# First FFN product of six chunks in three pairs by Strassen's scheme, with a new order

## The chip, the cores and the metric

The kernel runs on one core of a Trainium2 chip. The metric is the device time of one execution in microseconds; smaller is better. The engines are TensorE (PE: matmuls, and PEld for its weight loads), VectorE (DVE), ScalarE (ACT), GpSimd (POOL) and SyncE (SP, which issues the DMAs). All run at once and meet at semaphores.

## The reference

A block-local attention is followed by a feed-forward network (FFN):

```python
# q, k, v: (4, 8, 768, 64); local window of 16 positions, plus 24 block summaries
k_sum = k.reshape(B, H, nb, 32, D).max(axis=3)
v_sum = v.reshape(B, H, nb, 32, D).mean(axis=3)
scores_l = where(|i - j| < 16, q @ k.T / sqrt(D), -1e9)
scores_s = q @ k_sum.T / sqrt(D) + log(32)
a = softmax(concat([scores_l, scores_s], -1))
x = (a @ concat([v, v_sum])).transpose(0, 2, 1, 3).reshape(3072, 512)
h = x @ w_in                      # (3072, 512) @ (512, 2048)
g = h / (1 + exp(-h))
out = g @ w_out                   # (3072, 2048) @ (2048, 512)
```

## The kernel before

**Tiling.** The 3072 tokens are 24 stages of 128 (s, six to each of four batches b) and 12 chunks of 256 (c, two stages each). The 2048 columns of w_in are 8 pairs of 128-wide f tiles (f below is such a pair; d is the tile in it). The contraction of 512 is four blocks of 128 (ct). Operands of the large products are split in two float16 parts, high and low, and a product is three matmuls: high x high, high x low, low x high.

**Attention of a stage.** `job_qk` and `job_vs` load and split q, k and v (DMA, ScalarE, VectorE). `job_a` (L645) makes the scores of a quad on TensorE (L681), adds mask and takes the minimum on VectorE (L692), the exponential on ScalarE (L695), scales and splits p (L267 to L277), and transposes p by DMA (L737). `job_c` multiplies by v, two stages at once (AV, L770). `job_x` (L778) brings x from PSUM as high part (ScalarE, L267) and low part (VectorE, L274).

**FFN of a step (c, f)**, `job_f` (L898). First product, L916: 2 d x 4 ct x 3 terms = 24 matmuls of 128x128 weights by 256 tokens, into one PSUM bank h (d side by side). Then tanh on ScalarE (L930), (tanh + 1) * h on VectorE (L931, `stt`), a float16 cast on ScalarE (L935, `cast`) and its rest on GpSimd or VectorE (L277, `less`). Second product, L925: per half of the chunk 2 d x 3 terms = 6 matmuls of 512 columns, accumulated over all f in one bank per half. The bank h alternates between 0 and 1 from step to step. In chunks 0 and 1 f runs in two parts and the second product is in float32 for the first.

**Banks.** 0 and 1: h. 4, 5 (and 2, 3): outputs. From b = 1 on the scores use 2 and 6, AV 3 and 7.

**Order.** No engine's order is the source's. Every operation is given to `Plan.op` (L87) with the engines that may run it, its cost and the keys it reads and writes. `Plan.replay` (L179) reads the string `ORDER` (L1038): three base-36 digits for an operation's number times five plus its engine (pe, dma, dve, act, pool). Each engine issues its operations in that order and waits at each until its inputs and its bank are ready. The x of chunks c + 2 is made during the steps of chunk c.

## Time and profile before

| | us |
|---|---|
| median of 3 runs | 613.48 (613.43 to 615.46) |
| profiled execution, its own time | 614.0 |
| its span, first to last instruction | 612.3 |
| TensorE busy | 606.2 (99%), clock 1.00 |
| VectorE / ScalarE / GpSimd busy | 414.1 (68%) / 368.3 (60%) / 137.6 (22%) |

Busy time counts an instruction from its start to its end; matmuls overlap each other, so their mean duration is longer than the distance from one to the next. The chain of waits goes back from the last instruction, at each step to what released it. The span of the first step of chunks 2, 6, 8 and 10 to the next gives the stages used below: chunk 2 begins at 141.0 us, chunk 6 at 330.7, chunk 8 at 427.4, chunk 10 at 518.5.

### The profile page before, as it was taken

The page shows a single profiled execution, that of the slowest core. Times are in us where ns is not written, and L with a number is a line of the kernel's source. Part 1 is how long each engine was busy: PE and PEld are TensorE (multiplying, and loading weights), DVE is VectorE, ACT ScalarE, POOL GpSimd, SP SyncE. Part 2 cuts the span into 40 slices and gives each one's busy share as a digit, 9 for nine tenths or more (in the row PEclk, how much of TensorE's full clock was granted, in tenths as well). Part 3 has the DMA queues.
Part 4 walks back from the last instruction along what each step waited for, and adds up shares of the span by engine and source line. Part 5 has one row for each costly group of instructions (what it writes and reads, how often), then busy time and mean ns, then how long its engine had stood idle before and what let it go on. Part 6 is the DMA issues. An engine that isn't in the chain of part 4 may idle for free.

```text
span 612.3 us, 13657 instructions
## 1 busy us (share of the span) xinstructions
PE 606.2 (99%) x5229; PEld 417.3 (68%) x5229; DVE 414.1 (68%) x1135; ACT 368.3 (60%) x839; POOL 137.6 (22%) x191
## 2 busy tenths in 40 slices
...
GB/s 303 346 363 414 240 73 128 141 222 89 186 121 113 148 178 130 138 185 96 132 140 145 154 175 102 164 129 150 119 171 50 57 109 117 40 27 57 39 15 35
DMA packets 85701, 87.89 MB, mean 144 GB/s; under 512 B 66796, under 2 KB 69100, under 8 KB 83588
## 3 DMA queue, kind: packets, MB, share of 16 engines
...
## 4 chain that ended last, share of the span: by engine, by line
PE 96%; DMA 2%; ACT 0%; SPq 0%; DVE 0%; issue 0%; DVEq 0%
PE bank L925 42%; PE bank L916 41%; PE bank L770 4%; PE bank L681 3%; PE bank L754 1%; DMA wt<-in_w_dram 1%; DMA wt<-in_kF_dram 1%; PE bank L673 1%; PE bank L676 1%; PE bank L704 0%; PE bank L389 0%; PE bank L706 0%; PE bank L799 0%; ACT e L695 0%; PE bank L856 0%; PE bank L461 0%
## 5 line engine op out<-in xcount | busy, mean ns | idle before, releaser
L925 PE MATMUL bank<-wt,g 128*128 128x512 f16 (+2 forms) x1168 | 276.6, 383 | 0.0
L916 PE MATMUL bank<-xh,wt 128*128 128x256 f16 x1536 | 272.1, 273 | 0.0
L916 PEld LDWEIGHTS <-wt 128*128 128x128 f16 x2304 | 223.8, 98 | 50.1 <-issue 5.1
L916 PE MATMUL bank<-xl,wt 128*128 128x256 f16 x768 | 209.3, 273 | 0.0
L925 PEld LDWEIGHTS <-g 128*128 128x128 f16 x1104 | 105.8, 98 | 101.0 <-issue 0.9
L930 ACT ACTIVATE t<-bank,asc 128x512 f32<-128x512 f32 x96 | 65.8, 686 | 128.2 <-PE bank L916 123.9
L931 DVE SCALAR_TENSOR_TENSOR t<-t,bank 128x512 f32<-128x512 f32 x96 | 65.7, 685 | 105.1 <-ACT t L930 105.0
L695 ACT ACTIVATE e<-e,mx 128x182 f32<-128x182 f32 x192 | 83.8, 438 | 32.5 <-DVE mx L692 32.0
L277 POOL TENSOR_TENSOR g<-t,g 128x512 f16<-128x512 f32 x45 | 52.6, 1169 | 215.7 <-ACT g L935 115.2
L935 ACT CAST g<-t 128x512 f16<-128x512 f32 x88 | 54.1, 615 | 43.0 <-DVE t L931 40.3
L692 DVE CUSTOM_DVE_ANT_0 e<-bank,masks,qsc 128x182 f32<-128x182 f32 x144 | 54.7, 401 | 16.3 <-PE bank L681 15.7
L274 DVE SCALAR_TENSOR_TENSOR p<-e,sum,p 128x182 f16<-128x182 f32 x160 | 60.6, 423 | 5.3 <-ACT p L267 2.6
L269 POOL TENSOR_SCALAR p<-e,sum 128x182 f16<-128x182 f32 x61 | 29.0, 480 | 149.1 <-DVE sum L714 29.7
L277 DVE TENSOR_TENSOR g<-t,g 128x512 f16<-128x512 f32 x43 | 29.8, 692 | 15.6 <-ACT g L935 15.5
L695 ACT ACTIVATION_READ_ACCUMULATOR e<-e,mx 128x1 f32 x192 | 36.1, 188 | 0.0
L770 PEld LDWEIGHTS <-vv 128*64 128x64 f16 x800 | 22.7, 110 | 2.7 <-issue 2.1
L770 PE MATMUL bank<-tt,vv 128*64 128x128 f16 x800 | 24.4, 220 | 0.0
L267 ACT ACTIVATE p<-e,sum 128x182 f16<-128x182 f32 x50 | 20.8, 437 | 4.8 <-DVE sum L714 1.7
L681 PE MATMUL bank<-qk 64*128 64x182 f16 x432 | 23.3, 239 | 0.0
L274 DVE SCALAR_TENSOR_TENSOR vv<-raw,vsc,vv 128x1024 f16<-128x1024 f32 x17 | 21.7, 1278 | 1.3 <-ACT vv L267 1.3
L681 PEld LDWEIGHTS <-qk 64*128 64x128 f16 x432 | 15.5, 94 | 10.1 <-issue 9.5
L830 POOL TENSOR_SCALAR wt<-wt 128x1024 uint32<-128x1024 uint32 x12 | 13.9, 1157 | 35.4 <-DMA wt<-in_w_dram 17.2
...
## 6 DMA issues: line engine op xcount, KB each, us to landing
...
```

Source lines behind the costliest of these rows:

```text
L269: nc.gpsimd.tensor_scalar(out=out, in0=in_, scalar1=by, scalar2=0.0, op0=ALU.mult, op1=ALU.add)
L274: nc.vector.scalar_tensor_tensor(out=out, in0=in_, scalar=by, in1=less, op0=ALU.mult, op1=ALU.subtract)
L277: eng[e].tensor_tensor(out=out, in0=in0, in1=in1, op=ALU.subtract)
L681: nc.tensor.matmul(out=bank[pair_banks[o]][:, i * 256:i * 256 + NKEY], lhsT=ql_or_h[pr, hp, :], rhs=kst[pr, j, hp, :], start=(n == 0), sto ...
L692: plan.op({"dve": 258 if b == 0 else 323}, lambda e, i=i: nc.vector.tensor_tensor_reduce(out=et[:, i, :NKEY], in0=sc[:, i, :NKEY], in1=mas ...
L695: plan.op({"act": 431}, lambda e, i=i, h=h: nc.scalar.activation(out=et[:, i, :NKEY], in_=et[:, i, :NKEY], func=AF.Exp, scale=-1.0, bias=m ...
L770: nc.tensor.matmul(out=to[j * D:(j + 1) * D, i * P:(i + 1) * P], lhsT=vs[w][:, vi, h * D:(h + 1) * D], rhs=tt[:, j * 3 + blk, :], start=(n ...
L916: nc.tensor.matmul(out=h[:, d * CH:(d + 1) * CH], lhsT=wt[f, 0][:, part, d, ct * P:(ct + 1) * P], rhs=x[:, ct, :], start=(ct == 0 and q == ...
L925: nc.tensor.matmul(out=bank[to][:, :z0 - a0], lhsT=a[:, d * CH + u * P:d * CH + u * P + P], rhs=b[:, d, a0:z0], start=(opens and d == 0 an ...
L930: plan.op({"act": 640}, lambda e: nc.scalar.activation(out=t, in_=h, func=AF.Tanh, scale=asc_t[c // 3 % 2][:, f:f + 1]), r=[("bank", k), ( ...
L931: plan.op({"dve": 605}, lambda e: nc.vector.scalar_tensor_tensor(out=t, in0=t, scalar=1.0, in1=h, op0=ALU.add, op1=ALU.mult), r=[("bank", ...
L935: plan.op({"act": 540}, lambda e: nc.scalar.copy(out=gh, in_=t), r=[("t", j)], w=[("gh", n)], prio=at - TUNE["post"])
```

## The change

Chunks 6 to 11 run in pairs (6, 7), (8, 9), (10, 11). With the two chunks as rows, the halves of the contraction, and the two f tiles, h of a step is a 2 x 2 by 2 x 2 block product, and it is made by seven block products M1 to M7 of two ct each (6 matmuls a product) in place of eight, in `pair_f`. M1 and M5 go to the bank of the first chunk (left); `out5` copies M5 to SBUF and M1 to the second chunk's bank (right); M6 accumulates there; add6 writes the left bank's other half; M7 accumulates; add7 writes the right bank's other half; M2 and M3 finish the left bank, M4 the right. Then both banks go through the same tanh, `stt`, `cast`, `less` (`post`) and second products as before, with six g buffers in place of three. Pairs 6-7 and 8-9 use banks 0 and 1 in every step; pair 10-11 alternates with 6 and 7. `pair_x` also keeps x in float32 and makes four block sums with their high and low parts; `sum_w` makes four block sums of w_in for each f. From stage 16 on scores and AV share banks 6 and 7. All x of a pair is made before its first step, during the pair before.

The new ORDER has 2563 operations (2362 before): TensorE 518 (500), VectorE 927 (837), ScalarE 692 (615), GpSimd 181 (164), DMA 245 (246). Decoded, TensorE's order at the start of pair 6-7 (3.n is the n-th step of that pair, in the f order of PORDER; M15 is M1 and M5, M23 is M2 and M3; f2 a second product, a or b its chunk, 0 or 1 its half; sc scores):

```
c5.7f1_0 c5.7f1_1 c5.4f2_0 c5.5f2_0 s15av c5.6f2_0 c5.6f2_1 c5.7f2_0 c5.7f2_1 3.0M15 3.0unit
3.0M6 3.0M7 3.0M23 3.0M4 3.1M15 3.0f2a1 3.1M6 3.0f2a0 3.1M7 3.1M23 3.1M4 3.0f2b0 3.2M15 3.1f2a0
3.2M6 s16qtr 3.2M7 s16sc 3.1f2b0 3.2M4 s16sc 3.2M23 3.1f2a1 s17sc 3.0f2b1 3.3M15
```

VectorE's there (xlo: low part of x; v2: split of v; km: block maximum of k, for which L440 loads kF):

```
3.0out5 3.0add6 3.0add7 s15xlo s16v2 3.0stta s16km 3.0lessa 3.0sttb 3.1out5 s16km 3.1add6 s16km 3.1add7
```

TensorE's at the start of pair 8-9 and of pair 10-11, and its end:

```
3.7f2b0 s19av 3.6f2a1 3.5f2a0 3.7f2a1 s20sc 4.0M15 3.6f2a0 4.0M6 s20sc 4.0M7 4.0M23 4.0M4 3.7f2a0 4.1M15
s21sc 4.1M6 4.0f2b0 4.1M7 4.1M23 4.1M4 4.0f2a0 4.2M15
s23av 4.7f2a1 4.7f2b0 4.6f2b1 5.0M15 5.1M15 4.7f2a0 5.1unit 5.0M6
5.7M23 5.7M4 5.5f2b0 5.5f2b1 5.6f2a1 5.6f2a0 5.6f2b1 5.7f2a1 5.7f2a0 5.7f2b1 5.6f2b0 5.7f2b0
```

A step in the middle: `3.3M23 3.3M4 3.2f2a0 3.4M15 3.2f2a1 3.4M6 3.2f2b0 3.4M7 3.4M23 3.3f2a0 3.4M4`. Of the 16 `out5` in chunks 6 to 9 the order gives VectorE 3 in pair 6-7 and 4 in pair 8-9, and ScalarE 9.

The diff, cut to its core (ORDER's text left out):

```diff
+WCH = 6
+PORDER = (2, 3, 4, 5, 6, 7, 0, 1)
...
+        k = (2, 3, 4, 5)[m % 4] if m < 8 else (4, 5)[m % 2] if m < 16 else (6, 7)[m % 2] if b == 0 or s >= 2 * WCH + 4 else LATE_S[m % 2]
+        pair_banks = (k, k + 1) if b == 0 else LATE_S if s < 2 * WCH + 4 else (6, 7)
...
-        return 3 if s >= 2 * NSUP + 2 and s % 2 == 0 else 7
+        return (6 if s >= 2 * WCH + 4 else 3) if s >= 2 * NSUP + 2 and s % 2 == 0 else 7
...
+        if c >= WCH:
+            pair_x(s, prio)
+            return
...
+    def pair_x(s, prio):
...
+        plain = xw[j].rearrange("p (c t) -> p c t", c=NCT)[:, :, at]
+        plan.op({"act": 575, "dve": 600}, lambda e: times(e, plain, x3, by), r=[("bank", k)], w=[("xw", j, q, half) for q in range(2)], prio=prio, port=())
+        for q in ((0, 1) if j == 0 else (1,)):
+            n = 2 * j + q if j == 0 else 2
+            hi, lo = (xs_t[z][n][:, i, :, at] for i in range(2))
+            src = x3[:, 2 * q:2 * q + 2]
+            plan.op({"act": 365}, lambda e, hi=hi, src=src: times(e, hi, src, by), r=[("bank", k)], w=[("xs", z, n, half)], prio=prio)
+            plan.op({"dve": 370}, lambda e, hi=hi, lo=lo, src=src: rest_of(lo, src, by, hi), r=[("bank", k), ("xs", z, n, half)], w=[("xs", z, n, half, "low")], prio=prio, port=())
+        if s % 4 < 3:
+            return
+        a, b = (t.rearrange("p (q r) -> p q r", q=2) for t in xw)
+        steps = ((b[:, 1], b[:, 0], b[:, 1], ALU.add, (1, 1), 3), (b[:, 0], a[:, 0], b[:, 0], ALU.subtract, (1, 0), 5),
+                 (a[:, 0], b[:, 1], a[:, 0], ALU.subtract, (0, 0), 4), (a[:, 1], a[:, 1], a[:, 0], ALU.subtract, (0, 1), 6))
+        reads = (((1, 0),), ((0, 0),), ((1, 1),), ((0, 0),))
+        for (to, in0, in1, op, own, n), more in zip(steps, reads):
+            key = [("xw",) + own + (h,) for h in range(2)]
+            plan.op({"dve": 640, "pool": 1157}, lambda e, to=to, in0=in0, in1=in1, op=op: eng[e].tensor_tensor(out=to, in0=in0, in1=in1, op=op),
+                    r=[("xw",) + m + (h,) for m in more for h in range(2)], w=key, prio=prio)
+            hi, lo = (xs_t[z][n][:, i].rearrange("p c t -> p (c t)") for i in range(2))
+            plan.op({"act": 560}, lambda e, hi=hi, to=to: nc.scalar.copy(out=hi, in_=to), r=key, w=[("xs", z, n, h) for h in range(2)], prio=prio)
+            plan.op({"dve": 690, "pool": 1280}, lambda e, hi=hi, lo=lo, to=to: less(e, lo, to, hi), r=key + [("xs", z, n, h) for h in range(2)], w=[("xs", z, n, h, "low") for h in range(2)], prio=prio)
...
+    def sum_w(f, prio):
...
+            parts = [wt[f, 0][:, i].rearrange("p j c -> p (j c)") for i in range(2)]
+            plan.op({"pool": 2180, "dve": 1135}, lambda e: eng[e].tensor_tensor(out=wf, in0=parts[0], in1=parts[1], op=ALU.add), r=[("wh", f, 0), ("wl", f, 0)], w=own, prio=prio)
+        for out, in0, in1, op in ((b22, b22, b12, ALU.subtract), (b12, b12, b11, ALU.subtract), (b11, b22, b11, ALU.add), (b21, b21, b11, ALU.subtract)):
+            plan.op({"dve": 370, "pool": 640}, lambda e, out=out, in0=in0, in1=in1, op=op: eng[e].tensor_tensor(out=out, in0=in0, in1=in1, op=op), w=own, prio=prio)
+        r = 1.0 if f < NSUP else ur_t[:, f, 1:2]
+        hi, lo = (t.rearrange("p k c -> p (k c)") for t in wsum[f])
+        plan.op({"act": 1050}, lambda e: times(e, hi, wf, r), r=own + [("ur", f)], w=to + [("ws", f)], prio=prio)
+        plan.op({"dve": 1250}, lambda e: rest_of(lo, wf, r, hi), r=own + [("ur", f), ("ws", f)], w=to + [("wsl", f)], prio=prio)
...
+    need_c = {c: 2 * order.index((c, 0)) for c in range(WCH)}
+    for c in range(WCH, NCHUNK, 2):
+        need_c[c] = need_c[c + 1] = 2 * (len(order) + (c - WCH) * NFP)
...
+    def pair_f(i, c, n, f):
+        at = need_c[c] + 4 * n
+        z = c // 2 % 2
+        ka, kb = (6, 7) if c == NCHUNK - 2 and n % 2 else (0, 1)
...
+        m5 = m5_t[i % 2]
+        xs, ws = xs_t[z], wsum[f]
+        plain = [[wt[f, 0][:, part, d, q * 2 * P:(q + 1) * 2 * P] for part in range(2)] for d, q in ((0, 0), (0, 1), (1, 1))]
+        sums = [[ws[part][:, k] for part in range(2)] for k in (2, 0, 3, 1)]
+        terms = ((0, plain[0]), (1, plain[1]), (6, plain[2]), (2, sums[3]), (3, sums[0]), (4, sums[1]), (5, sums[2]))
+
+        def product(m, to, opens=False):
+            j, w2 = terms[m - 1]
+            for ct in range(2):
+                for q, (part, x) in enumerate(((0, 0), (0, 1), (1, 0))):
+                    nc.tensor.matmul(out=to, lhsT=w2[part][:, ct * P:(ct + 1) * P], rhs=xs[j][:, x, ct, :], start=(opens and ct == 0 and q == 0), stop=(ct == 1 and q == 2), skip_group_check=True)
...
+        left, right = (ha[:, :CH], ha[:, CH:]), (hb[:, :CH], hb[:, CH:])
+        if n < 2 and kb != 1 or i == 0:
+            plan.op({"pe": 110}, lambda e: nc.tensor.matmul(out=right[0], lhsT=unit[:, :P], rhs=unit, start=True, stop=True, skip_group_check=True), w=[("bank", kb)], prio=at, cols=256)
+
+        def both(e):
+            product(1, left[0], True)
+            product(5, left[1])
+
+        plan.op({"pe": 1310}, both, r=need(1, 5), w=[("bank", ka)], prio=at, cols=3072)
+
+        def out5(e):
+            copy(e, m5, left[1])
+            copy(e, right[0], left[0])
+
+        plan.op({"act": 740, "dve": 700}, out5, r=[("bank", ka)], w=[("m5", i % 2), ("bank", kb)], prio=at - TUNE["post"], port=())
+        plan.op({"pe": 655}, lambda e: product(6, right[0]), r=need(6), w=[("bank", kb)], prio=at, cols=1536)
+        plan.op({"dve": 350}, lambda e: nc.vector.tensor_tensor(out=left[1], in0=right[0], in1=m5, op=ALU.add), r=[("bank", kb), ("m5", i % 2)], w=[("bank", ka)], prio=at - TUNE["post"], port=())
+        plan.op({"pe": 655}, lambda e: product(7, right[0]), r=need(7), w=[("bank", kb), ("seven", i % 2)], prio=at, cols=1536)
+        plan.op({"dve": 350}, lambda e: nc.vector.tensor_tensor(out=right[1], in0=right[0], in1=m5, op=ALU.add), r=[("m5", i % 2)], w=[("bank", kb)], prio=at - TUNE["post"], port=())
+
+        def rest_a(e):
+            product(2, left[0])
+            product(3, left[1])
+
+        plan.op({"pe": 1310}, rest_a, r=need(2, 3) + [("seven", i % 2)], w=[("bank", ka)], prio=at, cols=3072)
+        plan.op({"pe": 655}, lambda e: product(4, right[0]), r=need(4), w=[("bank", kb)], prio=at, cols=1536)
+        opens, closes = n == 0, n == NFP - 1
+        gs = [post(c + u, (2 * i + u) % NT2, (2 * i + u) % 6, (ka, kb)[u], f, at) for u in range(2)]
+        for u in range(2):
+            gh, gl = gs[u]
+            j = (2 * i + u) % 6
+            ob = ((4, 5), (2, 3))[u]
...
+                def ffn2(e, gh=gh, gl=gl, to=ob[v], v=v):
+                    for d in range(2):
+                        for q, (a, b) in enumerate(((gh, 0), (gh, 1), (gl, 0))):
+                            nc.tensor.matmul(out=bank[to], lhsT=a[:, d * CH + v * P:d * CH + v * P + P], rhs=wt[f, 1][:, b][:, d, :], start=(opens and d == 0 and q == 0), stop=(closes and d == 1 and q == 2))
+
...
-        d = min([d for d in range(c + 1, NCHUNK) if slot[d] == slot[c]], default=None)
-        if d and f == (QF if c < NSUP else AHEAD):
+        d = c + 2 if c >= NSUP else 3 - c
+        if f == (QF if c < NSUP else AHEAD):
             job_stage(2 * d)
             job_attn(2 * d, True)
             job_stage(2 * d + 1)
...
+        if c >= NSUP and ((c - NSUP) * NFP + f) % (WCH - NSUP) == 0:
+            sum_w(PORDER[((c - NSUP) * NFP + f) // (WCH - NSUP)], 2 * i)
...
+    for c in range(WCH, NCHUNK, 2):
+        for n in range(NFP):
+            if c + 2 < NCHUNK:
+                s = 2 * c + 4 + n // 2
+                if n % 2 == 0:
+                    job_stage(s)
+                else:
+                    job_attn(s, True)
+                    if n % 4 == 3:
+                        job_out(s - 1, True)
+                        job_out(s, True)
+            pair_f(i, c, n, PORDER[n])
+            i += 1
```

## Rows read from the trace of the kernel before

**Rows 1.** The page: busy time of each engine, and the chain (sections 1 and 4).

```profile
PE 606.2 (99%) x5229; PEld 417.3 (68%) x5229; DVE 414.1 (68%) x1135; ACT 368.3 (60%) x839; POOL 137.6 (22%) x191
...
PE 96%; DMA 2%; ACT 0%; SPq 0%; DVE 0%; issue 0%; DVEq 0%
PE bank L925 42%; PE bank L916 41%; PE bank L770 4%; PE bank L681 3%; PE bank L754 1%; DMA wt<-in_w_dram 1%; DMA wt<-in_kF_dram 1%; PE bank L673 1%; PE bank L676 1%; PE bank L704 0%; PE bank L389 0%; PE bank L706 0%; PE bank L799 0%; ACT e L695 0%; PE bank L856 0%; PE bank L461 0%
```

**Rows 2.** The chain of waits, early: start us, length us, what.

```profile
20.54 0.04 issue
20.58 0.44 PE bank L704 x2
```

**Rows 3.** The same chain from 38.8 us to the end, by line.

```profile
by line: PE bank L925 45.2%; PE bank L916 44.3%; PE bank L770 4.1%; PE bank L681 3.6%; PE bank L676 0.6%; PE bank L754 0.3%; PE bank L461 0.2%; PE bank L523 0.2%; PE bank L673 0.2%; PE bank L704 0.2%; PE bank L706 0.2%; PE bank L856 0.1%; P
```

**Rows 4.** Pieces of the chain within chunks 2, 3 and 6.

```profile
184.53 0.58 PE bank L681 x12
185.11 1.42 PE bank L916 x12
...
203.45 1.29 PE bank L925 x6
...
211.28 2.35 PE bank L770 x80
...
330.65 2.62 PE bank L916 x24
```

**Rows 5.** All waits of TensorE: us in total, times, longest us.

```profile
PE bank L389 <- POOL ident masks.py:199: 1.4, 1, 1.4
PE bank L595 <- DMA wt<-in_v_dram: 0.9, 1, 0.9
PE bank L704 <- ACT e L695: 0.2, 1, 0.2
```

**Rows 6.** By stage: length, busy PE, PEld, DVE, ACT, POOL; clock, DMA share, GB/s.

```profile
38.83:155.00 116.17, 116.17 (x874) 78.51 (x874) 102.63 (x240) 95.97 (x195) 30.95 (x43) 1.00 0.61 193
140.97:330.65 189.68, 189.68 (x1701) 129.13 (x1699) 137.32 (x394) 115.14 (x276) 44.43 (x58) 1.00 0.55 139
330.65:427.40 96.75, 96.75 (x845) 65.70 (x844) 66.24 (x184) 55.35 (x134) 22.03 (x29) 1.00 0.57 149
427.40:518.50 91.10, 91.10 (x822) 62.29 (x820) 53.14 (x151) 49.87 (x122) 19.85 (x24) 1.00 0.47 105
518.50:600.90 82.40, 82.40 (x685) 60.36 (x684) 30.29 (x67) 28.66 (x56) 12.67 (x14) 1.00 0.14 33
```

**Rows 7.** Groups by line and form: count | busy us, mean ns | idle before.

```profile
L931 DVE SCALAR_TENSOR_TENSOR t<-t,bank 128x512 f32<-128x512 f32 x96 | 65.7, 685 | 105.1 <-ACT t L930 105.0
...
L277 DVE TENSOR_TENSOR g<-t,g 128x512 f16<-128x512 f32 x43 | 29.8, 692 | 15.6 <-ACT g L935 15.5
...
L274 DVE SCALAR_TENSOR_TENSOR vv<-raw,vsc,vv 128x1024 f16<-128x1024 f32 x17 | 21.7, 1278 | 1.3 <-ACT vv L267 1.3
...
L441 DVE TENSOR_REDUCE km<-raw 128x24 f32<-128x768 f32 x12 | 11.4, 946 | 2.8 <-DMA raw<-in_kF_dram 2.8
```

**Rows 8.** Timeline of a step in chunk 6: start us, length us, instruction.

```profile
343.42 0.27 PE L916 MATMUL bank<-xh,wt 128*128 128x256 f16 x1
...
343.79 0.69 ACT L930 ACTIVATE t<-bank,asc 128x512 f32<-128x512 f32 x1 [1.92 <-PE bank L916]
...
344.51 0.69 DVE L931 SCALAR_TENSOR_TENSOR t<-t,bank 128x512 f32<-128x512 f32 x1 [1.27 <-ACT t L930]
```

**Rows 9.** Timeline of VectorE: two neighbours in its queue.

```profile
205.58 0.69 DVE L277 TENSOR_TENSOR g<-t,g 128x512 f16<-128x512 f32 x1 [0.69 <-ACT g L935]
206.19 0.95 DVE L441 TENSOR_REDUCE km<-raw 128x24 f32<-128x768 f32 x1
```

**Rows 10.** Timeline: the kernel's last copy.

```profile
609.03 0.48 DVE L271 TENSOR_SCALAR raw<-bank,osc 128x256 f32<-128x256 f32 x1 [4.85 <-PE bank L925]
```

**Rows 11.** AV matmuls: duration min/median/max ns, first and last start us.

```profile
L770 PE MATMUL bank<-tt,vv x800: 219/219/243, 111.0 to 561.7; 128*64 128x128 f16 x160
```

More of the change, by code (lines that the diff above doesn't have):

```diff
@@ new lines, in sum_w @@
+    def sum_w(f, prio):
+        wf = plain_area(f, 0).bitcast(F32)
+        b11, b21, b12, b22 = (wf[:, i * CH:(i + 1) * CH] for i in range(4))
+        own = [("wv", f, 0), ("part", f)]
+        n = PORDER.index(f)
+        to = [("xr", i) for i in range(2)] if n == 0 else [("wv", PORDER[n - 1], 0)]
+        if f < NSUP:
+            parts = [wt[f, 0][:, i].rearrange("p j c -> p (j c)") for i in range(2)]
[6 more added lines that the diff above has]
+        plan.op({"dve": 1250}, lambda e: rest_of(lo, wf, r, hi), r=own + [("ur", f), ("ws", f)], w=to + [("wsl", f)], prio=prio)
@@ L891, in local_attn_ffn @@
     runs = [(c, first) for c in range(NSUP)] + [(c, rest) for c in reversed(range(NSUP))]
-    runs += [(c, first + rest) for c in range(NSUP, NCHUNK)]
+    runs += [(c, first + rest) for c in range(NSUP, WCH)]
     order = [(c, f) for c, fs in runs for f in fs]
     slot = [c if c < NSUP else NSUP - 1 - c % NSUP for c in range(NCHUNK)]
-    need_c = {c: 2 * order.index((c, 0)) for c in range(NCHUNK)}
+    need_c = {c: 2 * order.index((c, 0)) for c in range(WCH)}
+    for c in range(WCH, NCHUNK, 2):
+        need_c[c] = need_c[c + 1] = 2 * (len(order) + (c - WCH) * NFP)
     need_f = {f: 2 * min(i for i, cf in enumerate(order) if cf[1] == f) for f in range(NFP)}
@@ L961, in job_f, with post @@
             plan.op({"dma": 680}, lambda e, o=o, r0=r0: nc.sync.dma_start(out=out[r0:r0 + P, :], in_=o), r=[key[u]], prio=at - TUNE["out"])
+    def post(c, j, n, k, f, at):
+        h, t, g = bank[k], t_t[j], g_t[n]
+        gh, gl = (g.bitcast(F16)[:, i * 2 * CH:(i + 1) * 2 * CH] for i in range(2))
+        plan.op({"act": 640}, lambda e: nc.scalar.activation(out=t, in_=h, func=AF.Tanh, scale=asc_t[c // 3 % 2][:, f:f + 1]), r=[("bank", k), ("asc", c // 3 % 2, f)], w=[("t", j)], prio=at - TUNE["post"])
+        plan.op({"dve": 605}, lambda e: nc.vector.scalar_tensor_tensor(out=t, in0=t, scalar=1.0, in1=h, op0=ALU.add, op1=ALU.mult), r=[("bank", k)], w=[("t", j)], prio=at - TUNE["post"], port=())
+        plan.op({"act": 540}, lambda e: nc.scalar.copy(out=gh, in_=t), r=[("t", j)], w=[("gh", n)], prio=at - TUNE["post"])
+        plan.op({"pool": 1280, "dve": 690}, lambda e: less(e, gl, t, gh), r=[("t", j), ("gh", n)], w=[("gl", n)], prio=at - TUNE["post"])
+        return gh, gl
```

172 lines of the change are left out of this document (109 added, 63 removed).

## The prediction

> **What bounds the kernel now.** I read the page's first section, then the chain of waits, then TensorE's own waits and the stages, and last single instructions. The busy shares put TensorE at 99% with 606.2 us, VectorE and ScalarE at 68% and 60% [rows 1]. A busy TensorE could still be waiting, so the chain is read next: 96% of it is TensorE, nearly all on two lines, the second product (L925, 42%) and the first product (L916, 41%) [rows 1]. From 38.8 us, where the first product begins, to the last matmul, the chain is TensorE's alone; the one other entry is the copy after it [rows 3, 10]. In the stage of the change it is piece on piece: a whole chunk-and-f step of the first product takes 2.62 us (24 matmuls, 109.2 ns each), six matmuls of the second 1.29 to 1.30 us, the two AV stages 2.35 us, the scores of a quad 0.58 us, with nothing between them [rows 4]. TensorE's own list of waits has three entries, 2.5 us in all [rows 5]. The granted clock is 1.00 in every stage, the 2.4 GHz level, and what was run before each was dense [rows 6]. So time taken from TensorE's work in chunks 6 to 11 comes off the end, as long as the other engines deliver. That is the real question, because their work grows.
>
> **What goes.** Per f and pair of chunks, the first product was 2 chunks x 24 = 48 matmuls. The new one has seven products of 6 matmuls (two ct, three hi/lo terms), 42, of the same shape 128x128 by 128x256. 6 x 109.2 ns = 0.655 us, times 3 pairs x 8 f = 24: **-15.7 us** on TensorE. The second product, the scores and AV keep their counts.
>
> **What is added on TensorE.** Two seeding matmuls of 256 columns, 0.1 each at the pace above: **+0.2** (to 0.4, if each opens a gap of 0.11 as behind the scores [rows 4]).
>
> **What is added elsewhere, and its cover.** Sums of w_in blocks: eight f tiles, four block sums each, one split of 1024 columns (1.28 us on VectorE, by the `vv` row [rows 7]). The order puts them from before chunk 2 up to chunk 5. Wherever they lie on VectorE: 8 x 1.28 plus 32 x 0.48 at most (the 256-column VectorE row [rows 10] as the price of one), 25.6 us. VectorE was busy 137.3 of 189.7 us in chunks 2 to 5 [rows 6], so even the whole would fit (163). Cost nothing; cover is TensorE's 189.7 us of work there. If a post-step of the first product is delayed past its cover (the step's second product waits for it), it costs the delay: 0 to 3 us, I take 0.
>
> In chunks 6 to 9 VectorE gets, per pair of chunks, 16 adds of 256 columns (7.7 us), three or four of the out5 (two copies each, 0.88 us if the second starts 0.08 before the first has ended, as two neighbours on that engine do [rows 9]), and sums and splits of x net of what they replace (some 4 us): about 14.5. The attention of the last pair must now be done before it begins, where its AV matmuls went on until 562 us [rows 11]. VectorE is busy 30.3 us after 518.5 us, of which 16 steps' post (0.69 each and a `less` on about half, 0.35 [rows 7]) are 16.5: 13.8 us move forward. So 66.2 + 53.1 + 13.8 + 29 = 162 us of VectorE in 96.8 + 91.1 - 10.5 = 177 us [rows 6], **92%**, up from 64%. Cover remains, but thin, and VectorE runs its queue in order.
>
> **The new waits.** In each step M1 and M5 end, out5 copies, M6 accumulates, add6, M7, add7, then M4. TensorE's next instruction stands behind each. The handovers: ScalarE starts 0.10 us after the last matmul's end [rows 8]; TensorE 0.04 us after a releasing engine [rows 2]. So out5 holds M6 for 0.10 + 0.88 + 0.04 = 1.0 us (ends: 0.6, one 256-column copy alone; 1.5, two whole 512-column passes of 0.685 [rows 7]), and an add holds M7 for 0.10 + 0.48 + 0.04 = 0.6 us [rows 10] (ends 0.5 and 0.8, the 512-column `stt` being 0.69). Against that stands what the new order puts between (the stretches in the change section). A second product is 1.3 us, so one of them covers either. After M2 and M3 the bank needs tanh and `stt` before the next step's M1: 0.10 + 0.69 + 0.03 + 0.69 + 0.04 = 1.55 us [rows 8], and M4 (0.655) plus one second product (1.3) give 1.95. That is how nearly all steps stand. Those that do not:
>
> - *Start of pair 6-7.* The order has used up every second product of chunk 5, and step 3.0 runs bare. M6 waits 1.0, M7 0.6. Step 3.1's M1 needs `stta` of 3.0, which stands on VectorE behind add7, a 256-column split (about 0.4) and a V split (1.28) [rows 7]: it ends 2.85 us after M7, TensorE is free at 1.97: 0.9. Then 3.0's second product waits for a `less` behind a 0.95 us reduce [rows 7]: 0.2, and M6 of 3.1 for its out5 behind that: 0.15. Together **+2.9** (ends 1.0, if neighbours run early, and 5, if the kF loads between these also land late).
> - *Pair 8-9.* 4.0's M7 has scores of 0.58 as cover against 0.6, and 4.1's M6 has 0.58 against 1.0: **+0.5**. The x sums themselves (AV end to the low part of the first sum: 0.1 + 0.75 + 0.69 + two splits 0.9 + 0.69 = 3.1 us, estimated by the 512- and 256-column rows) have 4.5 us of second products and scores before them. At pair 10-11 3.9 us, against 3.1 to 3.9, since two more operations stand between. Nothing.
> - *Tail.* Now the last copy is 256 columns on VectorE, 0.48, and 2.8 us later the span ends [rows 10]. Then it is 512 columns: +0.25, and a larger store, +0 to 0.7: **+0.6**. The last f's post lies under five second products, 6.5 us against 3.2.
>
> All other steps: 16 of them beside attention, at 92% of VectorE. Before, no post came late [rows 5], with fewer meetings. I take **+1.0** (0.06 a step; ends 0 and 16 x 0.4).
>
> **Sum.** -15.7 + 0.2 + 2.9 + 0.5 + 0.6 + 1.0 = **-10.5 us**. The profiled execution took 614.0 us with a span of 612.3; the median of the runs, 613.48, lies 0.5 below it. I set the change against the median: 613.5 - 10.5 = **603.0 us** (span about 601.8, own time 603.5).
>
> **A rule that speaks against it.** In the kernel before two banks alternate between steps, and the trace shows one step's matmuls running through the other's tanh and `stt` [rows 8]. In pairs 6-7 and 8-9 both banks are filled in each step, so a step must wait for the read of the one before. The Trainium skill, "Perfetto Trace Analysis", section "Matmuls", says independent matmul groups should rotate through different PSUM banks so that reading one overlaps the next group's matmuls. The trace agrees for before; where it rules, the second rival below comes about.
>
> **The rivals.**
> 1. *The bare start is covered after all*, because copies and adds are shorter than my rows: only -15.7 + 0.2 + 0.6 + about 1 remain, 599.5 us. For it: 256-column operations on ScalarE have no row. Against it: three handovers in a chain without filler. Chance 0.17.
> 2. *VectorE's queue sets the pace in chunks 6 to 9* (the other side). Place: bank 0 between `stta` and the next M1, and M6 and M7 behind out5 and add6. If the covering second products are themselves late, nothing hides the 1.55 - 0.655 = 0.9 us, nor half of add6, 0.3: 1.2 us more for 16 steps, 19 us, and 603 - 1 + 19 = 621 us. It decides from (15.7 - 5.2)/16 = 0.65 us a step, where the gain is gone. For it: 92% and the one set of banks. Against it: an order that has 1.95 us against 1.55 in most steps, and a VectorE that at 103 of 116 us (38.8 to 155 us, 88%) let the chain stay on TensorE [rows 3, 6]. Chance 0.07.
> 3. *More starts late than I count*: sums of w and x push attention in chunks 2 to 5, or the kF loads at the pair's start land late; twice the stalls, +5, 608 us, with a tail to 612. For it: 16 stages of attention must be done by chunk 6, not 14 and a part of 15. Against it: VectorE at 72% there. Chance 0.16.
> 4. *The saving isn't there*: the 42 matmuls run slower than 109 ns each, since five short groups with waits replace two long ones. The chain shows 1.42 us instead of 1.31 for 12 matmuls behind the scores [rows 4]; 0.11 more at all 5 x 24 group starts is 13 us, 615. Against: L925 and L916 follow each other now without such a gap (1.29 us for six, 2.62 for 24). Chance 0.05.
>
> **How the numbers follow.** Forecast 0.55, with an own range of 600 to 606. The other chances as given. Telling faster from no change takes about 0.5%, 3.1 us (610.4 to 616.5). Faster: the forecast, rival 1 and most of rival 3 (0.55 + 0.17 + 0.15), 0.87; same (rival 4 and the end of rival 3) 0.06; slower (rival 2) 0.07. The range reaches from 598.5, below rival 1, to 610.5, over the most of rival 3.
>
> **What would show it.** L916's part and the new products: 2160 first-product matmuls instead of 2304, still 109 ns apart. TensorE's list of waits gains entries on out5 and the adds, most of their sum within 10 us of the start of pair 6-7; the chain there leaves TensorE for VectorE and ScalarE. Between steps 3.1 and 4.0, and all through pair 10-11, TensorE is packed. VectorE over 85% in chunks 6 to 9. A last copy of 0.7 us. I am wrong if TensorE waits over 0.3 us in most steps of chunks 6 to 9, if pair 6-7 begins later than it would by work alone (some 339 us: chunk 6 now begins at 330.7 us [rows 4], and 5 us of second products and 3 us of attention come before it), or if the gaps at M6 and M7 fail to appear at the bare start.

## Result and the profile after

605.92 us median of four runs (605.45 to 606.54) against 613.7 for the kernel before in the same session: ratio 0.987, 95% interval 0.985 to 0.989. The profiled executions took 605.51 us (span 603.8) and 614.0 (span 612.3), so the span fell by 8.5. Forecast were 603.0 us and -10.5. Among the experiments one execution, the one of e8 that was profiled, took 3493 us and is left out of e8's median; e12 is the same kernel again, for its trace.

The page of the kernel after, sections 1 and 4, answers to [rows 1]: TensorE still fills the chain. L982 is the first product of chunks 0 to 5, L1053 the Strassen products, L991 and L1101 the second product.

```profile
PE 594.7 (98%) x5052; PEld 400.1 (66%) x5052; DVE 462.7 (77%) x1237; ACT 403.3 (67%) x929; POOL 157.0 (26%) x206
...
PE 93%; DMA 3%; DVE 1%; ACT 1%; issue 0%; SPq 0%
```

All waits of TensorE after (us in total, times, longest), beside the three of [rows 5]. L1053 and L991 are TensorE's waiting lines; behind the arrow stands what released it: L265 copies of out5 on VectorE, L1033 the `stt`, L1079 add6, L269 ScalarE's scaling.

```profile
PE bank L391 <- POOL ident masks.py:199: 1.4, 1, 1.4
PE bank L1053 <- DVE bank L265: 1.0, 2, 0.7
PE bank L1053 <- DVE t L1033: 0.8, 1, 0.8
PE bank L991 <- ACT g L269: 0.8, 1, 0.8
PE bank L1053 <- DVE bank L1079: 0.5, 1, 0.5
PE bank L689 <- DVE km L457: 0.2, 1, 0.2
```

By stage (columns as in [rows 6]): chunks 2 to 5, then the pairs 6-7, 8-9 and 10-11. VectorE is busy 80.06 + 62.98 of 179.0 us in chunks 6 to 9, 80% (88% in pair 6-7).

```profile
146.30:339.60 193.30, 193.30 (x1786) 131.74 (x1784) 156.47 (x416) 135.58 (x324) 50.35 (x69) 1.00 0.61 151
339.60:430.40 90.80, 88.68 (x797) 58.86 (x795) 80.06 (x226) 64.89 (x160) 20.30 (x24) 1.00 0.56 149
430.40:518.60 88.20, 87.91 (x774) 58.60 (x773) 62.98 (x189) 52.76 (x141) 30.12 (x30) 1.00 0.38 93
518.60:599.70 81.10, 81.02 (x542) 52.82 (x540) 31.48 (x58) 26.26 (x46) 7.30 (x7) 1.00 0.06 22
```

The bare start in the timeline: M1, out5's two copies, M6 (0.75 idle before it), add6, M7 (0.53), the V split, tanh, `stta`, and M1 of 3.1 (0.84).

```profile
339.59 0.82 PE L1053 MATMUL bank<-wt 128*128 128x256 f16 x6
...
341.10 0.42 DVE L265 COPY xh<-bank 128x256 f32<-128x256 f32 x1
...
341.44 0.42 DVE L265 COPY bank<-bank 128x256 f32<-128x256 f32 x1
...
341.92 0.83 PE L1053 MATMUL bank<-wt,xr 128*128 128x256 f16 x6 [0.75 <-DVE bank L265]
...
342.79 0.43 DVE L1079 TENSOR_TENSOR bank<-bank,xh 128x256 f32<-128x256 f32 x1 [0.92 <-PE bank L1053]
...
343.27 0.50 PE L1053 MATMUL bank<-wt,xr 128*128 128x256 f16 x3 [0.53 <-DVE bank L1079]
...
344.81 1.27 DVE L276 SCALAR_TENSOR_TENSOR vv<-raw,vsc,vv 128x1024 f16<-128x1024 f32 x1
...
345.45 1.34 ACT L1032 ACTIVATE t<-bank,asc 128x512 f32<-128x512 f32 x2 [3.01 <-PE bank L1053]
...
346.17 0.69 DVE L1033 SCALAR_TENSOR_TENSOR t<-t,bank 128x512 f32<-128x512 f32 x1
...
346.91 1.47 PE L1053 MATMUL bank<-wt 128*128 128x256 f16 x12 [0.84 <-DVE t L1033]
```

**Where the time went.** One sum for all kernels, worked out from the starts of TensorE's matmuls: the time at which a matmul starts, less the work ahead of it at standard pace (109.2 ns for a first-product matmul, 216 for a second-product one, 29 for an AV one, 47 for a score, ...). What is left is time lost since the span began, in us; the table takes matmuls of no use (fillers, below) as lost too:

```
at us             60     160    331    355    430    last matmul
before          12.44  14.81  16.91  17.02  17.95  19.19
after           14.58  17.58  19.67  22.53  24.04  25.31
e4 early order  13.29  16.04  18.10  20.88  22.57  23.78
e10 late rows   15.14  18.22  20.31  21.17  24.22  25.46
e11 all         13.22  19.93  22.02  22.81  25.25  27.10
```

After against before: 2.1 lost by 60 us and 2.8 by 331; 2.8 more between 331 and 355, the bare start; 0.6 in all that follows. The work itself fell from 589.5 to 573.9 us. From the last copy's start to the end of the span it is 4.1 us (603.8 - 599.66) instead of 3.3 (612.3 - 609.03 [rows 10]). -15.6 + 2.8 + 2.8 + 0.6 + 0.9 = -8.5.

The first 40 us hold fillers: matmuls on a constant tile whose result nobody reads. The program issues them where its plan of the order expects TensorE to have nothing to do. The profile counts them as busy, so no list of waits has them. The kernel before has 47 and the kernel after 60, which is 8.1 and 9.7 us of busy time (e4 has 42, 7.3 us):

```profile
L389 PE MATMUL bank<-ident 128*128 128x256 bf16 x47 | 8.1, 336 | 1.4 <-POOL ident masks.py:199 1.4
```

```profile
L391 PE MATMUL bank<-ident 128*128 128x256 bf16 x60 | 9.7, 324 | 1.4 <-POOL ident masks.py:199 1.4
```

By 40 us, ahead of nearly all of the FFN, the kernel after has lost 0.9 more than the kernel before by the sum of the table. Whether TensorE would have waited as long without the fillers, no run shows.

### The profile page after: what moved, and what is told of

The parts are those of the page before. It is cut to its first block, busy times and chain, and to the rows that moved or that the text cites. A ratio compares the mean times of both kernels' runs of the same rounds, so it can differ in the third digit from the quotient of the medians.

```text
span 603.8 us, 13503 instructions
## 1 busy us (share of the span) xinstructions
PE 594.7 (98%) x5052; PEld 400.1 (66%) x5052; DVE 462.7 (77%) x1237; ACT 403.3 (67%) x929; POOL 157.0 (26%) x206
## 4 chain that ended last, share of the span: by engine, by line
PE 93%; DMA 3%; DVE 1%; ACT 1%; issue 0%; SPq 0%
PE bank L991 22%; PE bank L1101 21%; PE bank L982 19%; PE bank L1053 18%; PE bank L786 4%; PE bank L697 3%; DMA wt<-in_w_dram 1%; PE bank L689 1%; PE bank L770 1%; DMA wt<-in_kF_dram 1%; DMA raw<-in_vR_dram 1%; PE bank L720 1%; PE bank L391 1%; DMA out_dram<-raw 1%; PE bank L611 0%; PE bank L722 0%
## 5 line engine op out<-in xcount | busy, mean ns | idle before, releaser
L991 PE MATMUL bank<-wt,g 128*128 128x512 f16 (+1 forms) x544 | 141.9, 406 | 0.8 <-ACT g L269 0.8
L982 PE MATMUL bank<-xh,wt 128*128 128x256 f16 x768 | 136.2, 273 | 0.0
L982 PEld LDWEIGHTS <-wt 128*128 128x128 f16 x1152 | 111.5, 98 | 25.0 <-issue 3.8
L1053 PE MATMUL bank<-wt 128*128 128x256 f16 x936 | 114.4, 273 | 1.1 <-DVE t L1033 0.8
L1053 PEld LDWEIGHTS <-wt 128*128 128x128 f16 x936 | 90.8, 98 | 24.9 <-issue 1.7
L982 PE MATMUL bank<-xl,wt 128*128 128x256 f16 x384 | 104.7, 273 | 0.0
L991 PEld LDWEIGHTS <-g 128*128 128x128 f16 x480 | 45.8, 98 | 47.2 <-issue 0.2
L279 POOL TENSOR_TENSOR g<-t,g 128x512 f16<-128x512 f32 x34 | 39.4, 1159 | 123.5 <-ACT g L1034 47.7
L1101 PE MATMUL bank<-wt,g 128*128 128x512 f16 x288 | 69.3, 379 | 0.0
L1033 DVE SCALAR_TENSOR_TENSOR t<-t,bank 128x512 f32<-128x512 f32 x48 | 32.4, 684 | 22.1 <-ACT t L1032 21.8
L1101 PE MATMUL bank<-wt,xl 128*128 128x512 f16 x192 | 46.2, 379 | 0.0
L1101 PEld LDWEIGHTS <-g 128*128 128x128 f16 x288 | 27.6, 98 | 26.8
L269 ACT ACTIVATE p<-e,sum 128x182 f16<-128x182 f32 x76 | 31.3, 438 | 9.1 <-DMA tt<-p 3.3
L870 POOL TENSOR_TENSOR wt<-wt 128x256 f32<-128x256 f32 x20 | 14.5, 735 | 65.3 <-DVE wt L868 12.5
```

What stands on the lines that cost most here:

```text
L279: eng[e].tensor_tensor(out=out, in0=in0, in1=in1, op=ALU.subtract)
L982: nc.tensor.matmul(out=h[:, d * CH:(d + 1) * CH], lhsT=wt[f, 0][:, part, d, ct * P:(ct + 1) * P], rhs=x[:, ct, :], start=(ct == 0 and q == ...
L991: nc.tensor.matmul(out=bank[to][:, :z0 - a0], lhsT=a[:, d * CH + u * P:d * CH + u * P + P], rhs=b[:, d, a0:z0], start=(opens and d == 0 an ...
L1033: plan.op({"dve": 605}, lambda e: nc.vector.scalar_tensor_tensor(out=t, in0=t, scalar=1.0, in1=h, op0=ALU.add, op1=ALU.mult), r=[("bank", ...
L1053: nc.tensor.matmul(out=to, lhsT=w2[part][:, ct * P:(ct + 1) * P], rhs=xs[j][:, x, ct, :], start=(opens and ct == 0 and q == 0), stop=(ct = ...
L1101: nc.tensor.matmul(out=bank[to], lhsT=a[:, d * CH + v * P:d * CH + v * P + P], rhs=wt[f, 1][:, b][:, d, :], start=(opens and d == 0 and q ...
```

## The experiments

Theory: TensorE sets the end; Strassen takes its 15.7 us off, and what is missing is lost in three places, the start of the kernel, the bare start and the tail. Rivals: VectorE's queue paces chunks 6 to 9; the loss at the start has nothing to do with the order. The lengths of the pairs below are times from the first M1 of one pair to that of the next, and in the last pair to the last matmul.

**e1: a product twice.**

```diff
 def rest_a(e):
     product(2, left[0])
     product(3, left[1])
+    product(3, left[1])
```

> In every Strassen step M3 is computed twice (its six matmuls are issued again into the same columns, so 48 first-product matmuls a step as before the change; the output changes). Theory, TensorE sets the pace in chunks 6 to 11 and the saving is the 24 x 6 matmuls: +15.7 us on the kernel after, 621.4 us (620.5 to 622.2), each extra matmul 109 ns. Rival, VectorE's queue sets the pace in chunks 6 to 9: the extra matmuls hide there and only pair 10-11 pays, 8 x 0.655 = 5.2 us, 611 us.

620.98 us, ratio to before 1.011 (1.009 to 1.013); span 619.5. By stage:

```profile
339.60:435.70 96.10, 93.98 (x845) 63.61 (x844) 80.52 (x226) 64.88 (x160) 20.28 (x24) 1.00 0.52 142
435.70:529.10 93.40, 93.11 (x822) 63.26 (x821) 63.09 (x189) 52.83 (x141) 30.07 (x30) 1.00 0.34 86
529.10:615.40 86.30, 86.26 (x590) 57.53 (x588) 31.50 (x58) 26.20 (x46) 7.29 (x7) 1.00 0.06 21
```

Each pair grows by 5.24 us, eight times 0.655, with VectorE's busy time unchanged; the last matmul starts 15.7 later. TensorE is the bound in all three pairs, and the saving is there in full.

**e2 and e3: the adds twice and three times.** The add only writes the same sum again, so nothing of the computation changes.

```diff
-lambda e: nc.vector.tensor_tensor(out=left[1], in0=right[0], in1=m5, op=ALU.add)
+lambda e: [nc.vector.tensor_tensor(out=left[1], in0=right[0], in1=m5, op=ALU.add) for _ in range(2)]
...
```

> Each of the two adds of a step (add6, add7) is done twice, with the same operands and destination, so that the bank sums are not the reference's: 48 more VectorE passes of 0.43 us, 20.6 us on VectorE, 0.86 us a step. Theory, VectorE has cover except in the bare start of pair 6-7 and where pair 8-9 begins: M7 of 3.0 waits 0.43 longer, stta of 3.0 comes 0.4 later, M7 of 4.0 has 0.3 less cover: +1 to +2 us, 607.4 us. Rival, VectorE's queue sets the pace in chunks 6 to 9 or does so from 0.65 us a step: +3.4 us (16 x 0.21) to +13.8 us (16 x 0.86), 609.3 to 620 us, with TensorE waiting on adds and stt in most steps.

> As the run with the adds done twice, but three times: 41 us more on VectorE, 1.72 us a step. In pair 6-7 VectorE was busy 80.1 of 90.8 us, and 16 more passes make 93.8: there it must now be the bound. Theory: pair 6-7 grows by 3 to 7 us, pairs 8-9 (63.9 of 90.1) and 10-11 (30.6 of 79.2) hardly, so 612 us (609 to 616). Rival, VectorE decides from 0.65 us a step in chunks 6 to 9: 16 x 1.07 = 17 us, 623 us, half of it in pair 8-9.

e2: 609.74 us (ratio 0.993, 0.991 to 0.994), span +4.0; pairs +2.8, +1.1, +0.1. e3: 626.31 us (1.020, 1.018 to 1.021), span +20.3; pairs +8.5, +8.3, +3.2. Both went over the theory, and e2 into the rival's range. e2's waits of TensorE in pair 6-7:

```profile
PE bank L1053 <- DVE bank L1079: 1.4, 3, 1.0
PE bank L1053 <- DVE t L1033: 1.1, 1, 1.1
PE bank L1053 <- DVE bank L265: 0.7, 1, 0.7
PE bank L1053 <- DVE bank L1081: 0.2, 1, 0.2
```

e3 in pair 8-9, timeline: M6 of a step, the second product behind it, the tripled add6, and M7 0.17 late, though VectorE had been idle just before the add.

```profile
480.78 0.82 PE L1053 MATMUL bank<-wt 128*128 128x256 f16 x6
481.44 1.46 PE L1101 MATMUL bank<-wt,xh 128*128 128x512 f16 x6
483.06 2.12 PE L1053 MATMUL bank<-wt 128*128 128x256 f16 x18 [0.17 <-DVE bank L1079]
...
481.64 1.37 DVE L1079 TENSOR_TENSOR bank<-bank,xh 128x256 f32<-128x256 f32 x3 [0.57 <-PE bank L1053]
```

So a handover costs what it is longer than the piece that covers it. One add: the bare M7 above waits 0.53, of which 0.43 are the add. That is just under a quad of scores (0.58 [rows 4]). Two, some 1.0: over the scores, under a second product (1.3). Three, 1.4 to 1.5: over everything, and even pair 10-11 pays, where VectorE is busy 44.66 of 83.8 us.

The rival's numbers, though, come out about as well: from its 0.65 us a step (in the prediction the wait a step at which the gain is gone, in the expectations the load a step from which VectorE decides) it has 16 x 0.21 = 3.4 and 16 x 1.07 = 17.1 us, against 3.9 and 16.9 in pairs 6-7 and 8-9. So these two totals don't tell the theory from the rival. What speaks against the rival is the place: e2's nine waits lie in eight of the 16 steps (e3 does have one in each), VectorE was idle just before an add that came late, and pair 10-11, where the rival has nothing, pays 3.2 us in e3. My own +1 to +2 was short because it took only two uncovered handovers.

**e4: the early order of the kernel before.** The order list alone.

```diff
 ORDER = (
-    "1la1lm1m900400v01100l1lz1lh01f00r00b00h1m601k0...
+    (first 80 us: the order of the kernel before; up to 200 us moved to join; then as after)
```

> Only the order list differs from the kernel after: the first 80 us are issued in the order of the kernel before, and operations up to 200 us are moved so that the two orders join; the operations are the same. Theory, the 2.2 us that TensorE loses by 60 us (2.8 by 160 us) come from the new early order alone: -2.2 us, 603.7 us (603.0 to 604.6), and pair 6-7 begins near 337.3 us instead of 339.6. Rival, the loss has another cause (the sums of w, the weight loads' landing, a chip that was slower in that execution): no change, 605.9 us.

604.18 us (602.72, 603.58, 604.79, 605.63), ratio 0.984 (0.982 to 0.986, which overlaps that of the kernel after), span -1.9. Pair 6-7 begins at 337.93 us; in nine executions with the order of the kernel after it began at 339.1 to 341.2. The table says where: 1.3 less lost by 60 us, 1.5 by 160. e11 has the same early order and the same 13.2 at 60 us. But between 60 and 160 us the executions part. These rows are that stretch, first of after, then of e4, then of e11:

```profile
60.00:160.00 100.00, 99.95 (x730) 65.81 (x729) 90.19 (x219) 84.32 (x179) 28.42 (x44) 1.00 0.50 150
```

```profile
60.00:160.00 100.00, 100.00 (x745) 65.79 (x744) 92.67 (x222) 81.93 (x171) 33.47 (x54) 1.00 0.54 153
```

```profile
60.00:160.00 100.00, 96.80 (x710) 63.31 (x709) 89.60 (x210) 80.34 (x165) 31.90 (x52) 1.00 0.52 146
```

e11 idles 3.2 us there with e4's order. By 60 us the early order has lost 13.2 and 13.3 us in its two executions, the order of after 13.7 to 15.1 in ten (14.4 on the mean): so some 1.1 us are the order's. The remaining 1.7 of the 2.8 is no larger than what executions of one order differ by, and stays open. A run of the kernel before with the new early order, which would have been the counter-test, was not made.

**e5: the two copies of out5 swapped.**

```diff
-    copy(e, m5, left[1])
     copy(e, right[0], left[0])
+    copy(e, m5, left[1])
```

> The two copies of out5 change places: first M1's sum into bank B, which M6 waits for, then M5's into memory, which only the adds need. Nothing else differs from the kernel after. Theory, M6 of 3.0 and of 4.1 wait for the second of two copies of 0.42 us: M6 of 3.0 waits 0.35 instead of 0.75, M6 of 4.1 not at all instead of 0.28, the rest of the bare step comes 0.4 earlier: -0.6 us on the span of 603.8 (-0.4 to -0.9), 605.3 us. Rival, M6 is released by the whole of out5 (both copies on VectorE stand in one wait): no change.

605.48 us, ratio 0.986 (0.984 to 0.988). Pair 6-7 is 0.2 and pair 8-9 0.3 shorter; the start lost 1.0 more in the profiled execution, so its span shows nothing. 4.1's M6 waits no more; 3.0's gains 0.22, not 0.40:

```profile
341.88 0.27 PE L1065 MATMUL bank<-ident 128*128 128x256 bf16 x1
342.19 0.43 DVE L265 COPY bank<-bank 128x256 f32<-128x256 f32 x1
...
342.68 0.33 PEld L1053 LDWEIGHTS <-xr 128*128 128x128 f16 x4 [0.81 <-DVE bank L265]
342.68 0.50 PE L1053 MATMUL bank<-wt,xr 128*128 128x256 f16 x3 [0.53 <-ACT vv L269]
```

The copy into bank B now stands behind the seeding matmul into that bank. M6's matmul is put down to ScalarE, whose `vv` ended in the same moment; its weight load names the copy, which is the cause. The theory holds, at the lower end.

**e6: M2 before M7.**

```diff
-    plan.op({"pe": 655}, lambda e: product(7, right[0]), ...)
+    def two_seven(e):
+        product(2, left[0])
+        product(7, right[0])
+    plan.op({"pe": 1310}, two_seven, ...)
 def rest_a(e):
-    product(2, left[0])
     product(3, left[1])
```

> In every step M2 is issued between M6 and M7 instead of between M7 and M3, with the same products and banks. Theory, an add is a handover of 0.57 us (0.10 + 0.43 + 0.04): M2 (0.655) covers add6 where nothing did, M3 (0.655) still covers add7: M7 of 3.0 no longer waits 0.53, the rest of the packed steps stay packed: -0.5 us on the span of 603.8 (-0.3 to -0.8), 605.4 us. Rival, VectorE does not take up add7 at once, as its queue is in order, and M4 has now half the cover in each of 24 steps: 0.1 to 0.2 us a step, +2.4 to +4.8 us, 608 to 611 us.

607.26 us, ratio 0.989 (0.987 to 0.990); pairs +0.9, +0.2, +0.2. Neither came about as told; 0.9 of the longer time was lost in pair 6-7, and by 160 us that execution had already lost 1.6 more than the one of after. M6, add6, and what starts behind it is now M2:

```profile
343.53 0.83 PE L1053 MATMUL bank<-wt,xr 128*128 128x256 f16 x6 [0.75 <-DVE bank L265]
344.39 0.43 DVE L1079 TENSOR_TENSOR bank<-bank,xh 128x256 f32<-128x256 f32 x1 [0.92 <-PE bank L1053]
344.88 0.82 PE L1053 MATMUL bank<-wt 128*128 128x256 f16 x6 [0.53 <-DVE bank L1079]
...
348.99 0.71 PE L1053 MATMUL bank<-wt 128*128 128x256 f16 x5 [1.08 <-DVE t L1033]
```

M2 writes columns 0 to 255 of bank A, add6 columns 256 to 511 of the same bank, and M2 waits the same 0.53: it can't be add6's cover. Behind add7 only M3 is left as cover, and 3.1's M1 waits 0.24 longer than in after; the rest of the 0.9 stands in no list of waits. The Trainium skill ("PSUM — Partial Sum Buffer", section "PSUM bank collisions raise a hardware error") says that no two engines may access one bank in the same 32 partitions at once, and that the compiler puts a dependency between any two instructions that touch the same bank and partitions, whatever their columns. The trace agrees: M2 starts 0.06 us after the add's end, and has waited 0.53 for it. The expectation had overlooked it.

**e7 and e9: the last second product in halves.** e7 split the one that is issued third from the end, and shows nothing on the tail (605.17 us, 0.985, 0.984 to 0.987; pairs as in after). e9 splits the last. The condition in e7 (-) and in e9 (+), and the line that both add:

```diff
-ends = closes and c == NCHUNK - 2 and u == v == 1
+ends = closes and c == NCHUNK - 2 and u == 1 and v == 0
...
+for to, a0, z0, new in ((bank[to][:, :CH], 0, CH, False), (bank[0][:, :CH], CH, DM, True)) if ends else ((bank[to], 0, DM, opens),):
...
```

> The very last second product is split as in the kernel before: columns 0 to 255 end in their bank, columns 256 to 511 go to another bank, ScalarE takes the first bank while TensorE works on, and one VectorE pass of 256 columns adds the last part; the last row block is stored in two halves. Theory, the tail of 4.2 us from TensorE's last matmul to the end of the span goes back to the 3.3 us of the kernel before: -0.8 us on the span of 603.8 (-0.4 to -1.0), 605.1 us. Rival, the end is set by another store that was issued before: no change.

> As the run with the last second product in two halves, but for the second product that is issued last of all (chunk 11's first row block; the run before had split the one that is issued third from the end). Theory, the tail from TensorE's last matmul to the end of the span (4.6 us after its start in the kernel after, 3.3 us from the copy's start in the kernel before) shrinks as in the kernel before, the last copy to 0.48 us and the last store to half: -0.8 us on the span of 603.8 (-0.4 to -1.0), 605.1 us. Rival, the end is set by the fixed time from a store's issue to the end, whatever its size: -0.1 to -0.2 us only, the shorter copy.

605.62 us, 0.987 (0.985 to 0.989). The last copy of after, then of e9:

```profile
599.66 0.69 ACT L269 ACTIVATE raw<-bank,osc 128x512 f32<-128x512 f32 x1 [1.90 <-PE bank L1101]
```

```profile
599.48 0.48 DVE L1111 SCALAR_TENSOR_TENSOR raw<-bank,osc,raw 128x256 f32<-128x256 f32 x1 [10.23 <-ACT raw L269]
```

From its start to the end of the span (603.2) it is 3.7 us, against 4.1 and, before, 3.3. That would be half of the 0.9 from the width of the last copy and store. But e4, whose last copy and store are those of after, also has 3.7 us in its trace, so it isn't shown; the other half stays open as well.

**e8 and e12: one pair of banks in pair 10-11.**

```diff
-ka, kb = (6, 7) if c == NCHUNK - 2 and n % 2 else (0, 1)
+ka, kb = 0, 1
```

with the order rewritten from 510 us, so that a second product stands behind nearly every M5, M6 and M4 (M15 in the expectations is M1 with M5).

> In pair 10-11 every step uses the one pair of banks of pairs 6-9 instead of two pairs in turn, and the order from 510 us on is written anew for that: between the M4 of a step and the M15 of the next, and behind each M15 and M6, stands one second product. Theory, a handover (tanh and stt 1.55 us against 1.95 us of M4 and a second product; an add 0.57, out5 1.0 us against 1.3) is covered without a second pair of banks: only M7 of 5.0 has nothing between, +0.6 us, 606.5 us (605.9 to 607.5). Rival, the read of one step's bank must overlap the next step's matmuls in another bank: M15 of 5.1 to 5.7 each wait for the stt, 0.3 to 0.9 us a step, +2 to +6 us, 608 to 612 us.

> The same kernel as in the run with one pair of banks in pair 10-11, for its trace. Theory: about 606.7 us, and in pair 10-11 TensorE waits 0.6 us at M7 of 5.0 and not at any M15. Rival: the 0.8 us that it is longer than the kernel after is spread over the M15 of 5.1 to 5.7, about 0.1 us each.

606.73 and 606.49 us, ratio 0.988 (0.986 to 0.989, and 0.986 to 0.990). In e12's trace TensorE has one wait from 515 us to the end, M7 of 5.0:

```profile
PE bank L1053 <- DVE bank L1079: 0.6, 1, 0.6
```

The theory's 0.6 of the 0.8 us, at its place, and no first matmul of a step (M1) waits.

**e10: chunk 5's last rows through other buffers,** so that second products of chunk 5 can be held back.

```diff
 o = stg[:, u * DM:(u + 1) * DM]
+if c == WCH - 1:
+    o = xl_t[u].rearrange("p c t -> p (c t)").bitcast(F32)
+    key[u] = ("gh", 4 + u)
...
 ORDER = (
+    (between 318 and 390 us: c5.7f2_1 before M15, c5.6f2_0 before M6, c5.7f2_0 before 3.1's M15, ...)
```

> Chunk 5's output rows are copied to two buffers that held x of chunks 4 and 5 and that nobody reads any more, instead of to the load buffer that stage 16's kF load waits for; so second products of chunk 5 can be issued later, and between 318 and 390 us the order list is rewritten: one of them stands between M15 and M6 of 3.0 and one between M4 of 3.0 and M15 of 3.1. All else as in the kernel after. Theory, the 2.65 us of waits at the bare start are a lack of second products and nothing else: M6's 0.75 and the 0.84 of 3.1's M15 go, the waits behind them too, M7's 0.53 stays: -2.1 us, span 601.7, 603.8 us (603.2 to 604.6). Rival, VectorE at 88% in pair 6-7 is late by itself, and the wait moves to the next step: no change to -0.5 us, 605.6 us.

605.48 us, 0.986 (0.984 to 0.987), span 603.9: no gain on the whole. Yet the bare start is gone. Behind M1 and M5 come a second product, M6 without a wait, and M7 with 0.59:

```profile
339.06 1.46 PE L991 MATMUL bank<-wt,g 128*128 128x512 f16 x6
340.35 0.82 PE L1056 MATMUL bank<-wt,xr 128*128 128x256 f16 x6
341.76 0.81 PE L1056 MATMUL bank<-wt,xr 128*128 128x256 f16 x6 [0.59 <-DVE bank L1082]
```

From 331 to 355 us 0.9 is lost instead of 2.9: the theory's 2.0. Between 355 and 366 us 1.3 of it is given back (and 0.6 more than in after had been lost ahead of 331 us, nearly all of it by 60 us in the same order). The waits of that time that lead to TensorE's, and TensorE's matmul behind them (L477, of stage 16):

```profile
DVE qm L469 <- ACT raw L468: 2.2, 1, 2.2
...
ACT raw L468 <- DMA raw<-in_qF_dram: 1.4, 1, 1.4
```

```profile
358.86 0.71 PE L477 MATMUL bank<-ident,qm 128*128 128x128 f32 x4 [1.30 <-DVE qm L469]
```

ScalarE's |q| sum waits for a qF load, VectorE's sum for that, and TensorE for both. In the kernel after the same matmul starts at the same time, and without a wait:

```profile
358.90 0.71 PE L477 MATMUL bank<-ident,qm 128*128 128x128 f32 x4
```

So the load came no earlier although TensorE did, and TensorE waited for it. Not VectorE's load, as the rival had it, but a transfer; why it landed no earlier stays open.

**e11: all together** (e4, e5, e9, and e10 with the order rewritten from 318 to 460 us).

> The kernel after with the early order of the kernel before (first 80 us, operations up to 200 us rearranged), the late outputs of chunk 5 with the order rewritten from 318 to 460 us, out5's copies in the other order, and the last second product in halves. Theory, the parts add: -1.9 (early order), -2.1 (bare start), -0.3 (4.1's M6; 3.0's M6 is covered already), -0.8 (tail): -5.1 us on the span of 603.8, 600.8 us (600.0 to 602.0). Rival, the parts share one cause or VectorE becomes the bound in pair 6-7 once its waits are gone: -3 us, 602.9 us.

604.50 us (603.25 to 606.96), 0.985 (0.982 to 0.988). In the table the bare start costs 0.8 and 0.9 is given back by 430, but in the profiled execution TensorE idled 3.2 us between 60 and 160, and 0.6 more than after from 430 on. So the parts don't add to 5.1, and of all versions none is shown to beat the kernel after beyond the spread; e4's 604.18 is the lowest median.

## Why the prediction was right, and where not

- *The saving*, -15.7: right. 15.6 less work by the sum above, with 2160 first-product matmuls (1152 on L982, 1008 on L1053), and e1 brings it back by adding the matmuls again. L1053 runs at the pace of [rows 4].
- *Seeding matmuls*, +0.2: 0.11 each, as taken.
- *Bare start*, +2.9: 2.8, at the places named: M6 0.75 (1.0), M7 0.53 (0.6), 3.1's M1 0.84 (0.9). The reason for the last is only half right: the V split, which was to hold `stta`, ends at 346.08, but tanh ends at 346.14, so 3.1's M1 would wait for tanh and `stt` behind M2 and M3, with only M4 as cover, almost as long with an idle VectorE. That this part came out at 0.9 is luck. e10 shows that second products in the gaps remove it.
- *Pair 8-9 and the other steps*, +1.5: 0.6 by the last matmul; in the lists one wait of 0.3, at 4.1's M6. *Tail*, +0.6: 0.9.
- *VectorE at 92%*: 80%, so the sign of over 85% did not come. The term that was wrong is the attention. The prediction let the 13.8 us that VectorE spent on it behind 518.5 us come into chunks 6 to 9. Summed over the trace's instructions, only 1.5 us more of it stands there, and 3.1 more in chunks 2 to 5, while ScalarE does 8.9 and 10.4 us more of its scalings and splits. (VectorE's rise in chunks 2 to 5, 156.5 us instead of 137.3 [rows 6], is mainly the sums of w and the first pair's x, not attention.) Rival 2 fell with e1; e2 and e3 show that its price is right in kind (handovers longer than their cover), and their totals fit its numbers too. Rival 1 fell with the bare start's waits, rival 4 with e1. 605.9 lies towards rival 3 (608), but not for its reason: the late starts are ahead of chunk 2.
- *The sum, -10.5 against -8.5.* The term that failed is the one that was left at nothing ahead of chunk 6: only the sums of w were weighed, and they do cost nothing (between 160 and 331 us the kernels lose the same 2.1). But the order differs from the first load on, and by 60 us TensorE had lost 2.1 us more than before. Of these 0.9 were lost by 40 us, where the kernel after has 13 fillers more, and 0.8 are one wait: the first second product stands behind ScalarE's scaling, which stood behind a weight decode whose load had not landed. ScalarE's decode, its scaling, and the second product:

```profile
45.65 1.17 ACT L898 ACTIVATE wt<-wt 128x1024 f32<-128x1024 f32 x1 [0.95 <-DMA wt<-in_w_dram]
...
47.14 0.72 ACT L269 ACTIVATE g<-t,ur 128x512 f32<-128x512 f32 x1
...
47.91 1.13 PE L991 MATMUL bank<-wt,g 128*128 128x512 f32 x2 [0.77 <-ACT g L269]
```

  In e3, e7, e9 and e12, with the same order there, this wait is missing, so it is not the order's alone. The steady part is the 1.1 us of e4. The prediction's own sign for such a loss, pair 6-7 beginning later than some 339 us, was too coarse: it began at 339.6, and by the table that is 2.8 us later than with the losses of the kernel before. Of the total miss of 2.0 us, the 2.8 ahead of chunk 6 and 0.3 of the tail were partly hidden by the 0.9 that was taken too much for pair 8-9 and the other steps, which is luck.

- *The rule on banks* (the Trainium skill, "Perfetto Trace Analysis", section "Matmuls", rotate PSUM banks so that a read overlaps the next group). The traces agree where nothing else stands between: 3.1's M1 waits 0.84 us for the read of the bank that it writes. With a second product between, one pair of banks costs no wait at any M15 (e12), so rotation was not what this kernel lacked.
